# A planner's step times and due times reset, and some lower parts kept on VectorE, in a kernel of attention and two MLP layers

## The chip, the cores and the metric

The kernel runs on one core of a Trainium2 chip. The metric is the device time of one execution in microseconds. It has five engines here: TensorE (PE in the rows; its weight loads are PEld), VectorE (DVE), ScalarE (ACT), GpSimd (POOL) and SyncE (SP), which issues the DMAs. SBUF is the on-chip working memory, PSUM the memory that TensorE writes its products to, in banks.

## The reference

```python
def _attn_ref(q, k, v, g_q, g_k):          # (4, 12, 448, 64)
    q_n, k_n = rmsnorm(q, g_q), rmsnorm(k, g_k)
    scores = q_n @ k_n.T / sqrt(64)
    return softmax(scores) @ v

def _moe_ref(x, w_in, w_out):              # x: (1792, 768), w_in: (768, 2048), w_out: (2048, 768)
    h = x @ w_in
    return (h * sigmoid(h)) @ w_out

def _moe2_ref(x, w_in, w_out):
    return relu(x @ w_in) ** 2 @ w_out

def reference(**kwargs):
    x = attention of 4 batches and 12 heads, as (1792, 768)
    x = _moe_ref(x, moe_w_in, moe_w_out)
    return _moe2_ref(x, moe2_w_in, moe2_w_out)
```

Everything is float32.

## The kernel before

**Precision.** A float32 operand goes to TensorE as two parts: an upper part (a copy rounded to the matmul's type, `fp32r`, made by a CAST) and a lower part (what is left: the number less its upper part, a subtraction of two SBUF tiles, made by the helper `lower_part`, L558). One product takes three matmuls: upper by upper, upper by lower, lower by upper. In the tile names `gh` and `gl` are the upper and lower part of the hidden activations; `w`, `v`, `xb`, `yb`, `xc`, `part` and `W` hold both parts of weights, tokens and sums.

**Stages.** Attention over 24 pairs of heads takes the first 270 us and follows a fixed timetable. Then comes layer 1 (SiLU) until 736 us, in four quarters of the hidden columns; the first uses plain products (`up`, L1017, and `down`, L1201), the others a scheme with seven products in place of eight on half blocks (`seven`, L1104: nine matmuls of 448 columns in each product, into banks `t` or `pv`). Layer 2 (relu, squared) runs from 736 us. It handles the tokens in two halves, and in each half goes through eight groups of hidden columns: per group the products of the first matrix (L1104), the activation (ScalarE L1368 relu, L1374 square), the cast `gh` and the lower part `gl`, and then the second matrix into four `s` banks (384 columns, L1443) that VectorE adds to sums in SBUF (`acc`, L1462). In the second half, from 959 us on, the second matrix too uses seven products in most groups (class `products7`, L1568). For these the activation blocks are combined first into S1 to S4 (`h_sum`, L1500), and each of these sums is split by a cast (`h_hi`, on ScalarE or VectorE) and a lower part (`h_lo`) into tile `part` (S1, S2, S3) or `part` and `W` (S4). In TensorE's order of a group, product P4 (`s<-xb,gh`, nine matmuls) stands first, then P5 and P7 (`s<-xb,part`, nine each, from S1 and S3), then the others.

**What sets the order.** Apart from the attention's timetable, no order is written by hand. Each piece of work is a step with a set of engines that may do it, a time on each of them, and the steps that it needs. Class `Plan` makes the order: `forward` issues, of all steps that can go, the one that can start first, and of equal ones the one with the lower due time; `backward` works out due times from the end of that schedule; eight rounds, and the shortest schedule is issued. Table `DUE` adds an offset to the due time of each kind of step, by stage: `seg0` and `seg1` (layer 1 up to its second quarter and after), `end0` and `end1` (the two halves of layer 2, split at `self.turn`). The step times are formulas: `pe_t`, `dve_t`, `act_t`, `pool_t`, `any_t` (VectorE or GpSimd); `PROD` is one product of nine matmuls. An engine then works through its instructions strictly in the issued order, and waits on a semaphore where something that it needs is late.

**Names in the steps below.** `w_sum` (L1062, L1081) combines weight blocks in SBUF, `u_sum` (L1119) adds a product's bank to an SBUF tile, `join` (L1620) combines the sums at the end. Weights arrive as raw 8-byte words (`load_raw`, L913, L900), and ScalarE's `magnitude` and `low` (L920, L925) and VectorE's `merge` (L932) turn these into float32.

Of the kernel before, what the change touches and what calls it, by code (L numbers as in the profile page):

```python
# [98 lines left out]
class Step:  # L99
# [10 lines left out]
LAG = {"pe": 0.21, "act": 0.13, "dve": 0.12, "pool": 0.12, "sp": 1.9, "none": 0.0}  # L110
SELF = {"pe": 0.0, "act": 0.1, "dve": 0.1, "pool": 0.06, "sp": 1.9, "none": 0.0}
FORM = {"scores": "rows", "attend": "columns"}
SWITCH = 0.16
ENGINES = ("pe", "act", "dve", "pool", "sp", "none")
ROUNDS = 8
AHEAD = 25.0
DUE = {
    "end0": {"acc": 4.25, "down2": -1, "h_hi": 21.25, "h_lo": 3.75, "keep_parts2": -1.25, "load_y": -0.75, "p1_copy": 3.75, "prod": 0.25, "square": 1, "u_sum": -0.5, "w_hi2": -6, "w_lo2": -0.75, "w_sum": -0.75, "y_hi": 5.25, "y_lo": 4.25, "y_sum": -3.5},
    "end1": {"acc": 2, "down2": -11.25, "h_hi": 16, "h_lo": 2.5, "h_sum": -39.5, "join": 18, "keep_parts2": -11.75, "load_parts2": -2.25, "load_word2": 1.75, "load_y": 0.5, "p1_copy": 0.5, "prod": 2, "square": 21.25, "store": -1.25, "u_sum": -1, "w_hi2": 4.25, "w_sum": -4.5, "y_lo": -3, "y_sum": 2.5},
    "now": {"ident": 5.75, "swap_pools": -0.5},  # L120
    "seg0": {"add": -0.5, "down": 3, "g_hi": 0.5, "g_lo": 0.75, "keep": 10.25, "load_raw": -6, "load_y": 0.5, "low": 1, "magnitude": -2, "merge": -6, "out1": -1, "p1_copy": 4, "part": 0.5, "prod": 4.75, "silu": 0.5, "store_y": -1, "u_sum": 2.75, "up": 2.5, "w_hi": 4.5, "w_lo": 6.25, "w_sum": -2, "y_hi": 0.75, "y_lo": 1, "y_sum": 2},
    "seg1": {"add": -4.25, "down": -4.5, "g_hi": 2.25, "g_lo": 5, "keep2": 45.25, "load_raw2": 6, "load_word": -5.5, "load_y": -0.75, "low2": -1.5, "magnitude2": -3, "merge2": -4.5, "p1_copy": -6.25, "part": -3.75, "prod": -3.25, "silu": -5.75, "store_y": 7, "u_sum": 2.25, "w_hi": 1.75, "w_lo": 1, "w_sum": -3, "y_hi": 10, "y_lo": 0.75, "y_sum": 2.5},
}


class Plan:
# [47 lines left out]
    def link(self):  # L174


        for ring in self.rings.values():
            for b in ring:
                b.first = b.steps[0] if b.steps[0].nom is None else min(b.steps, key=lambda s: 1e9 if s.nom is None else s.nom)
                b.first.claims.append(b)  # L180
                if b.gate is not None:
                    b.first.needs[b.gate] = True
                for s in b.steps:
                    if s is not b.first:
                        s.needs.setdefault(b.first, False)
            ring.sort(key=lambda b: 1e9 if b.first.nom is None else b.first.nom)
            for n, b in enumerate(ring):
                b.turn = n
        pre = [dict() for _ in self.steps]
        for s in self.steps:  # L190
            for t, timed in s.needs.items():
                pre[s.n][t.n] = timed
            for b in s.claims:
                if b.turn:
                    t = b.ring[b.turn - 1].first
                    pre[s.n].setdefault(t.n, False)
                if b.turn >= b.n:
# [208 lines left out]
def kernel(  # L406
# [34 lines left out]
    step = plan.step  # L441
# [30 lines left out]
    def dve_t(n, rate=960.0, lock=False):  # L472
        return {"dve": (0.07 + n / rate, None, lock)}

    def pool_t(n, rate=474.0):
        return {"pool": (0.145 + n / rate, None, True)}

    def any_t(n, rate=474.0):
        return {**dve_t(n, 960.0, True), **pool_t(n, rate)}

    def copy_t(n):
# [2 lines left out]
    def pe_t(t):  # L484
        return {"pe": (t, None, False)}
# [13 lines left out]
    for n, src in enumerate((g_q, g_k)):  # L499
        for h in range(2):  # L500
# [4 lines left out]
                writes=[(graw, (n, h))],  # L505
# [10 lines left out]
    ident = sb([CP, CP], F32, "ident", 1)  # L516
# [35 lines left out]

        step(kind, when, copy_t(n), copy, reads=reads, writes=writes)

    def lower_part(kind, when, o, a, h, n, reads, writes, rate=474.0):

        step(
            kind, when, any_t(n, rate), lambda e: engine(e).tensor_tensor(o(), a(), h(), ALU.subtract),  # L558
            reads=reads, writes=writes,
        )  # L560

    def prepare(i):
# [88 lines left out]
        for n in range(2):  # L651
            n32 = sa([CP, NCH, 2, D], F32, "n")
            step(
                "norm", at, any_t(W2, 600.0),
                lambda e, n=n, n32=n32: engine(e).tensor_tensor(
                    n32.ap.rearrange("p c h d -> p h c d"),
                    qk.ap[:, n].rearrange("p (h c) d -> p h c d", h=2),
                    y.ap[:, n].rearrange("p (h c) -> p h c", h=2).unsqueeze(3).to_broadcast([CP, 2, NCH, D]),
                    ALU.mult),
                reads=[y, (qk, n)], writes=[n32],  # L660
            )
            plan.fix(i, "norm", j=n, at="dve" if i < 2 else "pool")
            pt = psum("t")

            def turn(e, n32=n32, pt=pt):
                for c in range(NCH):
                    nc.tensor.transpose(  # L667
                        pt.ap[:, c * CP:(c + 1) * CP], n32.ap[:, c].rearrange("p h d -> p (h d)"), ident.ap)

            step("turn_q", at, pe_t(0.384), turn, reads=[n32, ident], writes=[pt])  # L670
            plan.fix(i, "turn_q", j=n)

            def upper(e, n=n, pt=pt):
                o, a_ = T.ap[:, n, 0], pt.ap[:, :S]
# [32 lines left out]
    def weigh(i, T):  # L707
# [3 lines left out]
        for c in range(NCH):  # L711
# [15 lines left out]
            for j, pt in enumerate(pts):  # L727
                mx = sa([CP, 1], F32, "mx", 6)
                step(
                    "row_max", at, {"dve": (0.535, None, False)},  # L730
                    lambda e, pt=pt, mx=mx: nc.vector.tensor_reduce(  # L731
                        mx.ap, pt.ap[:CP, :S], AX.X, ALU.max, negate=True),
                    reads=[pt], writes=[mx],
                )
                plan.fix(i, "row_max", c, j)
                step(
                    "exp", at, {"act": (0.62, None, False)},
                    lambda e, j=j, c=c, pt=pt, mx=mx, E=E: nc.scalar.activation(  # L738
                        E.ap[:, j], pt.ap[:CP, :S], AF.Exp, bias=mx.ap, accum_out=sums.ap[:, j, c:c + 1]),
                    reads=[pt, mx], writes=[(E, j), (sums, (j, c))],  # L740
                )
                plan.fix(i, "exp", c, j)
                pe = psum("t")

                def turn(e, j=j, pe=pe, E=E):
                    for m in range(NCH):
                        nc.tensor.transpose(  # L747
                            pe.ap[:CP, m * CP:(m + 1) * CP], E.ap[:, j, m * CP:(m + 1) * CP], ident.ap)

                step("turn_e", at, pe_t(0.384), turn, reads=[(E, j), ident], writes=[pe])  # L750
                plan.fix(i, "turn_e", c, j)
                copy_step(
                    "e_copy", at, ECOPY[c][j], lambda c=c, j=j: PT[c // CT].ap[:, j * NCH:(j + 1) * NCH, c % CT, :],
                    lambda pe=pe: pe.ap[:CP, :S].rearrange("p (m t) -> p m t", t=CP), S, [pe], [(PT[c // CT], (c % CT, j))],
                )
                plan.fix(i, "e_copy", c, j)
        return PT, sums

    def attend(i, vr, PT, sums):
# [32 lines left out]
        for c2, pt in enumerate(PT):  # L792

            def products(e, c2=c2, pt=pt):
# [9 lines left out]
                        )  # L804

            step(
                "attend", at, pe_t(1.456), products,
                reads=[vr] + [(pt, (c, j)) for c in range(CT) for j in range(2)], writes=[(pv, c2)],
            )
            plan.fix(i, "attend", c2)  # L810
# [226 lines left out]
    FD = 2  # L1037
    halves = {}
    W3 = HC * P
    PROD = 9 * 0.2065  # L1040

    def view(b, a, c):

# [641 lines left out]
```

## Time and profile before

| | |
|---|---|
| median of 3 runs | 1165.32 us (1164.49, 1165.32, 1168.14) |
| the profiled execution | 1167.08 us |
| its span in the trace | 1165.3 us |
| TensorE busy | 1147.8 us, 99% of the span, 6817 matmuls |
| VectorE busy | 939.3 us, 81% |
| ScalarE busy | 632.3 us, 54% |
| GpSimd busy | 287.9 us, 25% |
| TensorE's granted clock, mean | 0.994 of full speed |

The busy share of a matmul includes its way through a pipeline, so that one matmul overlaps the next: the distance between the starts of two matmuls (their pitch) says how fast the engine goes. In the timeline one row can stand for several like instructions that follow each other (x2, x9); the bracket is the idle time of the engine ahead of it and what ended that. The code line is that of the helper which issues the instruction, so tiles tell more than lines.

### The profile page before, as it was taken

Reading aid. Unit: us, or ns where it says so; the run is one execution under the profiler, and the core shown is the slowest. Engines: PE = TensorE matmul, PEld = TensorE weight load, DVE = VectorE, ACT = ScalarE, POOL = GpSimd, SP = SyncE. Lnnn points to the kernel's source line nnn. Section 1 sums busy time; section 2 is a strip of 40 time slices with the busy share of each in tenths; the row PEclk is TensorE's granted clock in tenths of the full one; section 3 lists DMA queues with packets and bytes.
Section 4 is the critical chain, followed back from the end, with each engine's and each line's share of the span. In section 5 each row is a group of like instructions: output and inputs, shape, how many; then the busy total and the mean of one; then the engine's idle time right before and its main releaser. Section 6 shows DMA issues by size and latency. Waiting matters only on the chain.

```text
span 1165.3 us, 19244 instructions
## 1 busy us (share of the span) xinstructions
PE 1147.8 (99%) x6817; PEld 1018.8 (87%) x6817; DVE 939.3 (81%) x1685; ACT 632.3 (54%) x1290; POOL 287.9 (25%) x507
## 2 busy tenths in 40 slices
PE   7999999998999999999999999999999999999998
PEld 5777777777999999999999999999998999999997
DVE  7888888886876868996878698588888976888876
ACT  5999999985554444555535353543433535333321
POOL 4566676632000101210111021001121120122220
PEclk8999999999999999999999999999999999999999
DMA  6566768578855564778776849977777696555444
GB/s 175 94 103 115 105 109 111 99 125 175 275 167 185 172 212 133 263 236 273 244 238 209 272 145 329 337 271 261 286 264 260 217 378 230 177 176 190 164 163 135
DMA packets 142064, 235.22 MB, mean 202 GB/s; under 512 B 32016, under 2 KB 105744, under 8 KB 141968
## 3 DMA queue, kind: packets, MB, share of 16 engines
q1 hardware_dynamic: 141728, 233.80, 67.2%
q8 instruction: 54, 0.88, 0.3%
q14 instruction: 42, 0.34, 0.1%
q10 hardware_dynamic: 240, 0.20, 0.1%
HBM read 157.58 MB, written 76.37 MB: 201 GB/s over the span
## 4 chain that ended last, share of the span: by engine, by line
PE 91%; DVE 4%; ACT 2%; DMA 1%; issue 1%; SPq 0%; POOL 0%; ACTq 0%; DVEq 0%; POOLq 0%
PE t L1104 22%; PE s L1201 20%; PE s L1443 11%; PE pv L1104 9%; PE t L747 7%; PE pv L797 7%; PE s L720 6%; PE s L1568 6%; PE t L1017 2%; PE t L667 2%; DMA raw<-in_moe_w_out_dram 1%; DVE gg L1462 1%; DVE w L558 1%; DVE g L1119 0%; DVE g L1500 0%
## 5 line engine op out<-in xcount | busy, mean ns | idle before, releaser
L1201 PE MATMUL s<-gg,w 128*128 128x448 f32 x1152 | 240.4, 367 | 0.0
L1201 PEld LDWEIGHTS s<-gg,w 128*128 128x128 f32 x1152 | 216.2, 188 | 19.8 <-DVE g L1213 0.3
L1119 DVE TENSOR_TENSOR g<-t,g 128x448 f32<-128x448 f32 x180 | 108.8, 619 | 63.9 <-PE t L1104 53.1
L1443 PE MATMUL s<-w,gh 128*128 128x384 f32 (+1 forms) x564 | 143.0, 334 | 2.1 <-DVE gg L1462 1.1
L738 ACT ACTIVATE E<-s,mx 112x448 f32<-112x448 f32 x192 | 122.9, 653 | 13.7 <-ACT xf L537 7.9
L731 DVE TENSOR_REDUCE mx<-s 112x1 f32<-112x448 f32 x192 | 107.4, 611 | 14.4 <-PE s L720 14.1
L1462 DVE TENSOR_TENSOR gg<-s,gg 128x384 f32<-128x384 f32 (+1 forms) x197 | 102.6, 547 | 18.1 <-PE s L1443 17.7
L558 DVE TENSOR_TENSOR w<-W,w 128x768 fp32r<-128x768 f32 (+1 forms) x123 | 111.7, 917 | 4.2 <-ACT w L549 3.3
L1443 PEld LDWEIGHTS s<-w,gh 128*128 128x128 f32 x564 | 101.8, 188 | 4.0 <-DVE gg L1462 1.9
L1104 PE MATMUL t<-yb,w 128*128 128x448 f32 x468 | 103.1, 367 | 0.2 <-DVE w L558 0.2
L747 PEld LDWEIGHTS t<-ident,E 112*112 112x112 f32 x768 | 73.8, 134 | 32.5 <-issue 19.1
L549 ACT CAST w<-W 128x768 fp32r<-128x768 f32 (+1 forms) x74 | 54.9, 744 | 83.8 <-PE s L1201 31.9
L747 PE MATMUL t<-ident,E 112*112 112x112 f32 x768 | 94.7, 266 | 1.2 <-ACT E L738 1.2
L1368 ACT ACTIVATE g<-g 128x448 f32<-128x448 f32 x48 | 27.7, 578 | 124.6 <-DVE g L1119 124.1
L1443 PE MATMUL s<-w,gl 128*128 128x384 f32 (+1 forms) x282 | 94.3, 335 | 0.3 <-POOL gl L558 0.3
L1104 PEld LDWEIGHTS t<-yb,w 128*128 128x128 f32 x468 | 87.6, 188 | 8.1 <-DVE w L558 0.5
L797 PE MATMUL pv<-PT,vv 112*64 112x224 f32 x768 | 83.0, 359 | 0.1
L720 PE MATMUL s<-T 64*112 64x448 f32 x576 | 73.8, 388 | 1.3 <-ACT T L676 1.2
L1104 PE MATMUL pv<-xb,w 128*128 128x448 f32 x324 | 72.4, 367 | 0.0
L539 DVE COPY PT<-t 112x448 f32<-112x448 f32 x96 | 59.1, 618 | 11.6 <-PE t L747 11.5
L797 PEld LDWEIGHTS pv<-PT,vv 112*64 112x64 f32 x768 | 51.0, 136 | 20.0 <-ACT xf L537 0.3
L1104 PEld LDWEIGHTS pv<-xb,w 128*128 128x128 f32 x324 | 60.7, 188 | 5.5
(168 smaller groups left out, 2213.1 us busy)
## 6 DMA issues: line engine op xcount, KB each, us to landing
raw<-in_moe_w_in_dram SPq DMA_DIRECT2D x32, 768.0 KB
raw<-in_moe_w_out_dram SPq DMA_DIRECT2D x24, 512.0 KB
raw<-in_moe_w_out_dram SPq DMA_DIRECT2D x16, 768.0 KB
su<-w SPq DMA_DIRECT2D x16, 768.0 KB
w<-su SPq DMA_DIRECT2D x16, 768.0 KB
xf<-y SPq DMA_DIRECT2D x48, 224.0 KB
xf<-x SPq DMA_DIRECT2D x39, 224.0 KB
ki<-W SPq DMA_DIRECT2D x16, 384.0 KB
```

Source lines behind the costliest of these rows:

```text
L558: kind, when, any_t(n, rate), lambda e: engine(e).tensor_tensor(o(), a(), h(), ALU.subtract),
L720: nc.tensor.matmul(pts[j].ap[:CP, :S], T.ap[r, 0, a, c * CP:(c + 1) * CP], T.ap[r, 1, b_], start=(k_ == 0), stop=(k_ == 2),)
L731: lambda e, pt=pt, mx=mx: nc.vector.tensor_reduce(mx.ap, pt.ap[:CP, :S], AX.X, ALU.max, negate=True),
L738: lambda e, j=j, c=c, pt=pt, mx=mx, E=E: nc.scalar.activation(E.ap[:, j], pt.ap[:CP, :S], AF.Exp, bias=mx.ap, accum_out=sums.ap[:, j, c:c ...
L747: nc.tensor.transpose(pe.ap[:CP, m * CP:(m + 1) * CP], E.ap[:, j, m * CP:(m + 1) * CP], ident.ap)
L797: nc.tensor.matmul(pv.ap[j * D:(j + 1) * D, c2 * CT * CP:(c2 + 1) * CT * CP], vr.ap[:, j * NCH + m, :], pt.ap[:, j * NCH + m].rearrange("p ...
L1104: nc.tensor.matmul(pt.ap[:, :S], w_()[:, c0 + c, :], view(b, a, c)(), start=(start and c == 0 and k == 0), stop=(c == HC - 1 and k == 2), ...
L1119: lambda e: nc.vector.tensor_tensor(o.ap, pt.ap[:, :S], a.ap, ALU.add),
L1201: nc.tensor.matmul(pt.ap[:, :S], w_()[:, f, :], gg.ap[:, k, a, f, :], start=(f == 0 and n == 0), stop=(f == HQ - 1 and n == 2),)
L1443: nc.tensor.matmul(pt.ap[:, :en], g.ap[:, fi, c0:c0 + P], w_()[:, 0, e0:e0 + en], start=(n == 0), stop=(n == 5),)
L1462: "acc", at, dve_t(n), lambda e: nc.vector.tensor_tensor(o(), pt.ap[:, :n], o(), ALU.add),
L1568: nc.tensor.matmul(pt.ap[:, :NH], a[i][0](m), b[j][0](), start=(start and k == 0), stop=(k == 2), skip_group_check=True,)
```

## The change

All of it is in the planner's numbers and in one rule; the arithmetic is the same, and TensorE has as many matmuls as before.

- GpSimd's step time goes from 0.145 us and 474 elements per us to 0.1 us and 415 elements per us.
- `PROD` goes from 9 × 0.2065 to 9 × 0.2028 us; a turn of the attention from 0.384 to 0.406, an attended product from 1.456 to 1.512, and the time that a change of matmul form adds from 0.16 to 0.13. Since the nominal position of a step is made of such times, the point `self.turn` moves with them.
- A lower part of an activation (`h_lo`) in the last half of layer 2 can't go to GpSimd any more.
- All offsets of `DUE` are others.

```diff
-SWITCH = 0.16
+SWITCH = 0.13
...
 DUE = {
-    "end0": {"acc": 4.25, "down2": -1, "h_hi": 21.25, "h_lo": 3.75, "keep_parts2": -1.25, "load_y": -0.75, "p1_copy": 3.75, "prod": 0.25, "square": 1, "u_sum": -0.5, "w_hi2": -6, "w_lo2": -0.75, "w_sum": -0.75, "y_hi": 5.25, "y_lo": 4.25, "y_sum": -3.5},
+    "end0": {"acc": -0.5, "h_hi": 18.5, "h_lo": 3.25, "keep_parts2": 10.75, "load_word2": -0.5, "load_y": -0.75, "p1_copy": -1.75, "relu": -0.25, "square": 8.5, "u_sum": 2, "w_hi2": 1, "w_lo2": -0.5, "w_sum": 2.75, "y_hi": 3.5, "y_lo": -1, "y_sum": -4},
...
 }
@@ link
+        for s in self.steps:
+            if s.kind == "h_lo" and s.when[1] >= self.turn:
+                s.on.pop("pool", None)
+                s.at = "dve"
...
-    def pool_t(n, rate=474.0):
-        return {"pool": (0.145 + n / rate, None, True)}
+    def pool_t(n, rate=415.0):
+        return {"pool": (0.1 + n / rate, None, True)}
 
-    def any_t(n, rate=474.0):
+    def any_t(n, rate=415.0):
         return {**dve_t(n, 960.0, True), **pool_t(n, rate)}
...
-            step("turn_q", at, pe_t(0.384), turn, reads=[n32, ident], writes=[pt])
+            step("turn_q", at, pe_t(0.406), turn, reads=[n32, ident], writes=[pt])
...
-                step("turn_e", at, pe_t(0.384), turn, reads=[(E, j), ident], writes=[pe])
+                step("turn_e", at, pe_t(0.406), turn, reads=[(E, j), ident], writes=[pe])
...
-                "attend", at, pe_t(1.456), products,
+                "attend", at, pe_t(1.512), products,
...
-    PROD = 9 * 0.2065
+    PROD = 9 * 0.2028
```

The attention's order on TensorE is the same in both programs; from layer 1 on, runs of equal products change places, and helpers move between VectorE, GpSimd and ScalarE. Three places follow. The code lines of the changed kernel are higher by four from the new loop on (L1104 is L1108, L558 is L562, L1081 is L1085, L1443 is L1447, L1462 is L1466, L1500 is L1504, L1568 is L1572).

Place one, VectorE in the first half of layer 2, about 874 to 883 us in the trace of before: the weight sums, the lower parts and the bank sums that free the banks of a run `s<-w,gh` (L1443). Before:

```order
L1119 TENSOR_TENSOR g<-t,g 128x448
L1062 TENSOR_TENSOR W<-W 128x384
L551 CAST v<-W 128x384
L1062 TENSOR_TENSOR W<-W 128x384
L558 TENSOR_TENSOR gl<-g,gh 128x448
L1081 TENSOR_TENSOR W<-W 128x384
L1462 TENSOR_TENSOR gg<-s,gg 128x384
L1081 TENSOR_TENSOR W<-W 128x384
L558 TENSOR_TENSOR gl<-g,gh 128x448
L1462 TENSOR_TENSOR gg<-s,gg 128x384 x2
```

and now:

```order
L1123 TENSOR_TENSOR g<-t,g 128x448 x2
L1066 TENSOR_TENSOR W<-W 128x384
L1380 TENSOR_TENSOR g<-g 128x448
L1066 TENSOR_TENSOR W<-W 128x384
L562 TENSOR_TENSOR v<-W,v 128x384
L1085 TENSOR_TENSOR W<-W 128x384
L1466 TENSOR_TENSOR gg<-s,gg 128x384 x2
L562 TENSOR_TENSOR gl<-g,gh 128x448
L1085 TENSOR_TENSOR W<-W 128x384
L1466 TENSOR_TENSOR gg<-s,gg 128x384 x3
```

Two bank sums (L1462, now L1466) stand now right behind the first of the two `w_sum` L1081 (now L1085); before, `gl` stood ahead of that `w_sum`, and one bank sum behind it. The GpSimd instruction that ran beside the first `w_sum` (the lower part of `w`) is still issued there, after a `gl`; the lower part of `v` has moved from GpSimd to VectorE.

Place two, TensorE at about 929 to 932 us, where a run of the second matrix begins (`gh` and `gl` are the activations of the group). Before:

```order
L1104 MATMUL t<-xc,w 128x448 x9
L1104 MATMUL t<-part,w 128x448 x9
L1443 MATMUL s<-w,gh 128x384 x2
L1443 MATMUL s<-w,gl 128x384
L1443 MATMUL s<-w,gh 128x384 x2
```

and now:

```order
L1108 MATMUL t<-xc,w 128x448 x9
L1108 MATMUL t<-part,w 128x448 x9
L1108 MATMUL pv<-raw,w 128x448 x9
L1447 MATMUL s<-w,gh 128x384 x2
L1447 MATMUL s<-w,gl 128x384
```

A product of nine matmuls on `raw` and `w` now stands ahead of the first matmul that reads `gl`.

Place three, VectorE in the second group of the last half, about 985 to 991 us: the sums S1 and S2 (L1500), the bank sums and the lower parts in `part`. Before:

```order
L1500 TENSOR_TENSOR g<-g 128x384
L558 TENSOR_TENSOR gl<-g,gh 128x64
L1119 TENSOR_TENSOR g<-t,g 128x448
L1500 TENSOR_TENSOR g<-g 128x384
L1462 TENSOR_TENSOR gg<-s,gg 128x384
L558 TENSOR_TENSOR part<-g,part 128x384
L1462 TENSOR_TENSOR gg<-s,gg 128x384 x5
```

and now:

```order
L1504 TENSOR_TENSOR g<-g 128x384
L562 TENSOR_TENSOR gl<-g,gh 128x64
L1123 TENSOR_TENSOR g<-t,g 128x448
L1504 TENSOR_TENSOR g<-g 128x384
L1466 TENSOR_TENSOR gg<-s,gg 128x384 x3
L562 TENSOR_TENSOR part<-g,part 128x384 x2
```

The lower part of S1 comes two bank sums later, and that of S2, which GpSimd made, stands behind it. In the fifth group of that half the order on TensorE changes too. Before, nine products on `raw` stood between P4 and P5:

```order
L1568 MATMUL s<-xb,gh 128x384
L1568 MATMUL s<-W,gh 128x384
L1568 MATMUL s<-xb,gl 128x384
L1104 MATMUL pv<-raw,w 128x448 x9
L1568 MATMUL s<-xb,part 128x384 x18
L1568 MATMUL s<-w,gh 128x384 x2
```

and now P5 follows P4, and they come behind it:

```order
L1572 MATMUL s<-xb,gh 128x384
L1572 MATMUL s<-W,gh 128x384
L1572 MATMUL s<-xb,gl 128x384
L1572 MATMUL s<-xb,part 128x384 x9
L1108 MATMUL pv<-raw,w 128x448 x9
L1572 MATMUL s<-xb,part 128x384 x9
```

## Rows read from the trace of the kernel before

**Rows 1.** Page: busy time, the chain that ended last, one costly group

```profile
PE 1147.8 (99%) x6817; PEld 1018.8 (87%) x6817; DVE 939.3 (81%) x1685; ACT 632.3 (54%) x1290; POOL 287.9 (25%) x507
...
PE 91%; DVE 4%; ACT 2%; DMA 1%; issue 1%; SPq 0%; POOL 0%; ACTq 0%; DVEq 0%; POOLq 0%
...
L1119 DVE TENSOR_TENSOR g<-t,g 128x448 f32<-128x448 f32 x180 | 108.8, 619 | 63.9 <-PE t L1104 53.1
```

**Rows 2.** Windows: length; busy us (count) of PE, PEld, DVE, ACT, POOL; PE clock, DMA share, GB/s

```profile
265.00:300.00 35.00, 31.92 (x174) 27.40 (x171) 21.01 (x35) 17.80 (x33) 4.23 (x3) 0.95 0.79 187
300.00:736.00 436.00, 436.00 (x2131) 399.52 (x2130) 348.78 (x587) 215.25 (x349) 50.11 (x35) 1.00 0.69 227
870.00:885.00 15.00, 13.58 (x70) 12.14 (x69) 15.00 (x21) 6.47 (x12) 5.02 (x4) 1.00 0.74 272
960.00:1126.00 166.00, 164.83 (x862) 154.53 (x861) 132.84 (x260) 64.41 (x124) 31.52 (x30) 1.00 0.55 194
```

**Rows 3.** TensorE's waits: us in total, times, longest us

```profile
PE t L1017 <- ACT g L1029: 3.0, 1, 3.0
...
PE s L1568 <- DVE part L558: 1.1, 2, 0.8
```

**Rows 4.** Chain of waits: start us, us, engine and line, count

```profile
306.78 26.04 PE s L1201 x126
...
512.00 5.64 PE t L1104 x27
...
529.80 24.32 PE s L1201 x120
```

**Rows 5.** Timeline 270 to 284 us: start, length, work [idle before]

```profile
280.20 0.66 ACT L920 ACTIVATE W<-raw 128x512 f32<-128x512 f32 x1 [7.97 <-DMA raw<-in_moe_w_out_dram]
...
283.31 2.58 PE L1017 MATMUL t<-xc,w 128*128 128x448 f32 x9 [3.00 <-ACT g L1029]
```

**Rows 6.** Timeline 870 to 882 us: VectorE beside GpSimd

```profile
870.97 2.77 DVE L558 TENSOR_TENSOR w<-W,w 128x768 fp32r<-128x768 f32 x2
...
871.59 1.34 POOL L558 TENSOR_TENSOR gl<-g,gh 128x448 fp32r<-128x448 f32 x1 [0.96 <-ACT gh L549]
...
878.24 1.83 POOL L558 TENSOR_TENSOR w<-W,w 128x768 fp32r<-128x768 f32 x1 [0.35 <-ACT w L549]
878.29 2.20 DVE L1081 TENSOR_TENSOR W<-W 128x384 f32<-128x384 f32 x1
...
881.01 0.61 PE L1443 MATMUL s<-w,gh 128*128 128x384 f32 x2 [1.13 <-DVE gg L1462]
```

**Rows 7.** Timeline at 930 us: TensorE waits for a lower part

```profile
930.17 1.30 POOL L558 TENSOR_TENSOR gl<-g,gh 128x448 fp32r<-128x448 f32 x1 [2.47 <-issue]
...
930.70 0.52 PE L1443 MATMUL s<-w,gh 128*128 128x384 f32 x2
...
931.52 0.45 PE L1443 MATMUL s<-w,gl 128*128 128x384 f32 x1 [0.30 <-POOL gl L558]
```

**Rows 8.** Timeline 988 to 992 us: the second group of products

```profile
988.31 0.55 DVE L558 TENSOR_TENSOR part<-g,part 128x384 fp32r<-128x384 f32 x1
...
988.55 1.18 POOL L558 TENSOR_TENSOR part<-g,part 128x384 fp32r<-128x384 f32 x1 [33.52 <-ACT part L549]
988.77 2.41 DVE L1462 TENSOR_TENSOR gg<-s,gg 128x384 f32<-128x384 f32 x5
...
988.91 3.06 PE L1568 MATMUL s<-xb,part 128*128 128x384 f32 x16 [0.82 <-DVE part L558]
```

**Rows 9.** Timeline 1068 to 1073 us: the fifth group

```profile
1068.39 0.55 DVE L558 TENSOR_TENSOR part<-g,part 128x384 fp32r<-128x384 f32 x1
...
1068.79 1.17 POOL L558 TENSOR_TENSOR gl<-g,gh 128x448 fp32r<-128x448 f32 x1 [1.78 <-ACT gh L549]
...
1069.21 3.48 PE L1568 MATMUL s<-xb,part 128*128 128x384 f32 x18
1069.33 1.04 DVE L1500 TENSOR_TENSOR g<-g 128x384 f32<-128x384 f32 x1
```

More of the change, by code (lines that the diff above doesn't have):

```diff
@@ L117 @@
 DUE = {
-    "end0": {"acc": 4.25, "down2": -1, "h_hi": 21.25, "h_lo": 3.75, "keep_parts2": -1.25, "load_y": -0.75, "p1_copy": 3.75, "prod": 0.25, "square": 1, "u_sum": -0.5, "w_hi2": -6, "w_lo2": -0.75, "w_sum": -0.75, "y_hi": 5.25, "y_lo": 4.25, "y_sum": -3.5},
-    "end1": {"acc": 2, "down2": -11.25, "h_hi": 16, "h_lo": 2.5, "h_sum": -39.5, "join": 18, "keep_parts2": -11.75, "load_parts2": -2.25, "load_word2": 1.75, "load_y": 0.5, "p1_copy": 0.5, "prod": 2, "square": 21.25, "store": -1.25, "u_sum": -1, "w_hi2": 4.25, "w_sum": -4.5, "y_lo": -3, "y_sum": 2.5},
@@ L120 @@
-    "now": {"ident": 5.75, "swap_pools": -0.5},
-    "seg0": {"add": -0.5, "down": 3, "g_hi": 0.5, "g_lo": 0.75, "keep": 10.25, "load_raw": -6, "load_y": 0.5, "low": 1, "magnitude": -2, "merge": -6, "out1": -1, "p1_copy": 4, "part": 0.5, "prod": 4.75, "silu": 0.5, "store_y": -1, "u_sum": 2.75, "up": 2.5, "w_hi": 4.5, "w_lo": 6.25, "w_sum": -2, "y_hi": 0.75, "y_lo": 1, "y_sum": 2},
-    "seg1": {"add": -4.25, "down": -4.5, "g_hi": 2.25, "g_lo": 5, "keep2": 45.25, "load_raw2": 6, "load_word": -5.5, "load_y": -0.75, "low2": -1.5, "magnitude2": -3, "merge2": -4.5, "p1_copy": -6.25, "part": -3.75, "prod": -3.25, "silu": -5.75, "store_y": 7, "u_sum": 2.25, "w_hi": 1.75, "w_lo": 1, "w_sum": -3, "y_hi": 10, "y_lo": 0.75, "y_sum": 2.5},
+    "end0": {"acc": -0.5, "h_hi": 18.5, "h_lo": 3.25, "keep_parts2": 10.75, "load_word2": -0.5, "load_y": -0.75, "p1_copy": -1.75, "relu": -0.25, "square": 8.5, "u_sum": 2, "w_hi2": 1, "w_lo2": -0.5, "w_sum": 2.75, "y_hi": 3.5, "y_lo": -1, "y_sum": -4},
@@ new lines @@
+    "end1": {"acc": -4.5, "down2": -20.25, "h_hi": 15.25, "h_lo": 3.75, "h_sum": -5, "join": -0.75, "load_parts2": 0.5, "load_word2": -5.25, "load_y": 2.75, "p1_copy": 2, "prod": -0.75, "square": 50.25, "store": -3.75, "u_sum": 4, "w_hi2": -3.25, "w_lo2": -19.25, "w_sum": -2, "y_hi": -2.75, "y_lo": -0.25, "y_sum": -8.75},
+    "now": {"ident": 7.5, "swap_pools": -3},
+    "seg0": {"add": -0.75, "down": 4, "g_hi": 3, "g_lo": 2, "keep": -4.5, "load_raw": -29.75, "low": 6, "magnitude": 6.25, "merge": -5.5, "out1": 1.75, "p1_copy": 3, "part": -1, "prod": 5, "silu": -2.25, "store_y": -0.25, "u_sum": 2.75, "up": -1.75, "w_hi": 7.25, "w_sum": 6, "y_hi": -15, "y_lo": -0.25, "y_sum": -2.5},
@@ L123 @@
+    "seg1": {"add": -1, "down": -5.75, "g_hi": 6.5, "keep2": 55.75, "load_raw2": -0.25, "load_word": 7.75, "load_y": -0.5, "low2": 24.5, "magnitude2": 2.25, "merge2": -5.75, "out1": -1.75, "p1_copy": 1.25, "part": 11.5, "prod": -4, "silu": -11.5, "u_sum": 1.75, "w_hi": -2.5, "w_lo": 1.75, "y_hi": 6.25, "y_lo": -1.5, "y_sum": 10.75},
 }
@@ L553, in upper_part, with lower_part @@
         step(kind, when, copy_t(n), copy, reads=reads, writes=writes)
-    def lower_part(kind, when, o, a, h, n, reads, writes, rate=474.0):
+    def lower_part(kind, when, o, a, h, n, reads, writes, rate=415.0):
         step(
```

## The prediction

> **What bounds the kernel now.** I read the page first. TensorE is busy for 1147.8 of 1165.3 us, and the chain that ended last is TensorE for 91% [rows 1]. So only two things can move the time: the 17.5 us in which TensorE does nothing, and the pace at which it works. GpSimd's 25% and VectorE's 81% count only where TensorE waits for them. The list of TensorE's waits comes next: the largest behind the attention is one of 3.0 us at the start of layer 1, then the lower parts of the sums S1 (1.1 us in two places) [rows 3]. Then I cut the span into windows at the stages: from 300 to 736 us, which is layer 1 without its start, TensorE is never idle; the idle time stands at the start of layer 1 (35.00 − 31.92 = 3.1 us), in one stretch of the first half of layer 2 (870 to 885: 1.4 us) and in small pieces in the last half (960 to 1126: 1.2 us) [rows 2].
>
> The chain of waits shows the pace. 126 matmuls of layer 1 take 26.04 us, which is 206.7 ns from one to the next, and 120 of the same line take 24.32, which is 202.7 [rows 4]. The turn is the run that starts at 512.00: 27 matmuls in 5.64, 208.9 each, just behind a short wait for a bank; all runs of the chain behind it up to 736 have the quicker pace. The granted clock is 1.00 at both. So layer 1 ran about half at either pace, as its mean says: 436.00 us for 2131 matmuls are 204.6 ns [rows 2]. The reason isn't in the trace, and the order of instructions doesn't tell which pace a kernel gets.
>
> **The change, part by part.** The profiled execution took 1167.08 us, 1.8 more than its span and 1.76 above the median 1165.32; I work in its time and take 1.76 off at the end.
>
> Attention: TensorE's order is unchanged, its fixed timetable too. 0.
>
> Start of layer 1. TensorE waits because silu, which empties a bank, stands on ScalarE behind the conversion of a weight block that lands at about 280.2 (ScalarE idle for 7.97 us ahead of it); TensorE goes on at 283.31 after 3.00 us [rows 5]. In the new order the same two conversions and the table load still stand ahead of silu. 0, with −3 (the block lands in time) and +3 (a DMA is put ahead of it) as bounds.
>
> First half of layer 2, place one. At 878.24 GpSimd begins a lower part of 1.83 us, and VectorE's `w_sum`, begun at 878.29, takes 2.20 instead of the 0.55 that a subtraction of that size takes elsewhere [rows 6, 8]: it is held until GpSimd has ended. The bank sums behind it come late, and TensorE loses 1.13 at 881.01. A smaller loss ahead of it is of the same kind: two lower parts of `w` take 2.77 on VectorE beside GpSimd's `gl` (1.34). In the new order two bank sums stand right behind the first `w_sum`, so a VectorE held later holds back no bank before the fourth group of six matmuls, and the earlier `gl` has left GpSimd. The window's idle time is 15.00 − 13.58 = 1.42 us [rows 2], and refilling the pipeline after a wait costs about 0.17 more each (below). Of about 1.7 I count 1.6 as gone: **−1.6** (bounds: 0, if GpSimd's two instructions, now back to back, hold VectorE at another place; −1.8).
>
> Here a rule can be weighed against the row. The Trainium skill (SBUF — State Buffer, Who interferes with whom) says that a VectorE instruction with two inputs in SBUF and a GpSimd instruction that reads SBUF share a port pair, and that the later one is blocked until the earlier has ended. This trace agrees: 878.29 + 2.20 = 880.49 is 1.83 behind 878.24 plus about 0.4 [rows 6]. The rule also speaks against the change: four `h_sum` and six more `w_sum` now go to GpSimd, and each may hold VectorE for up to its own length. By that alone VectorE would lose up to 10 us (an estimate: ten times about 1.0, the GpSimd time of 384 columns being 1.18 in rows 8); by the rows only what a bank sum or an S1 waits for reaches TensorE.
>
> Place two. At 930.70 two matmuls start, and the third, which reads `gl` from GpSimd (930.17, 1.30 us), starts 0.82 later instead of 2 × 0.173 = 0.35 (0.173 is the pitch of 384 columns: 18 take 3.48 in rows 9, less the tail) [rows 7]. The loss is 0.47, of which 0.30 is idle and 0.17 the refilled pipeline. Now nine matmuls (9 × 0.2067 = 1.86 us) stand ahead of it. **−0.5**; nothing takes its place, since `gl` is then over a microsecond early.
>
> Last half of layer 2: seven groups with P4, P5, P7. P4's nine matmuls take 1.56 us, and the third of P5 needs the lower part of S1, so that this has to be ready 1.9 us after P4's start unless other products stand between. A further 384-column instruction on VectorE costs (2.41 − 0.55)/4 = 0.465 us [rows 8].
> - Group 2: two bank sums more ahead of the lower part, which ends at 988.31 + 0.55 now: 2 × 0.465 = **+0.9** on a wait that already costs 0.82 + 0.17.
> - Group 1: same order on TensorE, one more cast of 384 columns on ScalarE ahead of what it waits for. No row shows such a cast; I take an estimate of about VectorE's time for that size: **+0.4** (bounds 0 and 0.9).
> - Group 5: before, nine products on `raw` covered P5 (it began 0.17 late at 1069.21). Now they come behind P5's first nine. VectorE has to do `u_sum` (0.62 [rows 1]), `h_sum`, three bank sums, a small `gl` (0.14, estimated from its 64 columns) and the lower part: 0.4 + 0.54 + 5 × 0.465 + 0.14 = 3.4 against the 1.9 needed. A wait of 1.5 takes the place of 0.4: **+1.1**.
> - Groups 3, 4, 6, 7: fills of nine products stand between P4 and P5 or P5 and P7, as in group 5 before. There `h_sum` took 1.04 beside GpSimd's `gl` (1068.79, 1.17) instead of 0.55 [rows 9], and the groups lost 0.1 to 0.4. GpSimd's lower parts are gone there, so the holding goes with them: **−1.1** for the four.
>
> Together +1.3. VectorE gets 14 more lower parts of 384 columns (6.5 us), about five `gl` (2.7) and five small ones (0.7), and loses four `h_sum` (1.9): 8.0 us more over seven groups, 1.1 each. It was busy for 132.84 of 166.00 us there [rows 2]; with this about 84%. The cover is the 5 us that it is idle in a group.
>
> Other small waits of layer 2 (two of under 0.5, one near 1145) stand behind the same work in both orders: 0, ±0.5. Pace: 0.
>
> Sum: −1.6 − 0.5 + 1.3 = −0.8. 1167.08 − 0.8 − 1.76 = **1164.5 us**, no change that this measurement can tell: that takes over 0.3%, 3.5 us.
>
> **Rivals.**
> 1. *Layer 1 at the slow pace to its end.* The short wait at 512 came from a bank sum behind other work on VectorE; in the new order that sum (`u_sum`, L1119) stands ahead of it, so this wait may be missing and the pace not turn. 2131 × 206.7 ns = 440.4 in place of 436.0: +4.4, 1168.9. Against it: any other short wait does the same.
> 2. *Layer 1 at the quick pace from its start.* 2131 × 202.7 = 431.9: −4.1, 1160.4. For it: the 3.00 us wait is just ahead. Against it: in this trace that wait was followed by the slow pace.
> 3. *Nearly all waits of layer 2 go*, since GpSimd's times are now nearer to its rows (1.17 for 448 columns in rows 9 against 0.145 + 448/474 = 1.09 planned). Then the +2.4 of groups 1, 2, 5 don't come and 1.4 more go: 1160.7. Against it: the new order shows these groups' lower parts late.
> 4. *VectorE becomes the bound of the last half.* If the lower part of S1 is later than 1.9 us after P4's start in all seven groups, each waits 1.5: 10.5 in place of the 5.2 that my sum holds: +1.3 on a loss of 3.9 before (1.1 in groups 1 and 2 each, 0.1 in 3, 0.4 in each of 4 to 7, counted along the timeline as in rows 8 and 9). That is +5.3, and 1169.8. For it: 84% busy, the two groups above. Against it: the fills in four groups.
> 5. *The start of layer 1 moves* by up to 3 us either way: 1161.5 or 1167.5.
>
> **How the numbers follow.** Forecast 0.44 (within 0.3% 0.37, faster 0.05, slower 0.02), rival 1 0.17 (slower 0.09, same 0.08), rival 2 0.15 (faster 0.14), rival 3 0.11 (faster 0.10), rival 4 0.10 (slower), rival 5 0.03. Faster 0.30, same 0.47, slower 0.23. The range runs from below rivals 2 and 3 (each less a microsecond of the unknown waits) to rival 4: 1159.0 to 1169.8.
>
> **What would show it.** The chain of the changed kernel should have TensorE without idle time at 870 to 885 and at 930; waits of `s<-xb,part` for `part` of about 1.5 to 2 us in groups 1, 2 and 5 and of nearly nothing in the others; `w_sum` on VectorE without a 2.20; the 3.0 us of L1017 as before. The pace of L1201 says which of rivals 1 and 2 is there. I am wrong if those three waits are missing or stand in all groups, if new waits appear in layer 1, or if the mean of the 2131 matmuls leaves 204.6 by more than a nanosecond.

## The result and the profile after

The changed kernel takes 1172.51 us (median of 11 runs, 1166.39 to 1183.60), the kernel before beside it 1165.44 (11 runs, 1159.56 to 1169.30). The ratio is 1.0061, with a 95% interval of 1.0035 to 1.0088: slower by 0.6%, and above the range that was predicted (1159.0 to 1169.8). The profiled execution took 1169.55 us, 2.5 more than that of before, with a span of 1167.7.

The page of the changed kernel, as [rows 1]: TensorE's busy time and its share of the chain are lower.

```profile
PE 1146.3 (98%) x6817; PEld 1022.5 (88%) x6817; DVE 943.4 (81%) x1703; ACT 630.7 (54%) x1292; POOL 260.5 (22%) x487
...
PE 85%; ACT 5%; DMA 4%; DVE 4%; issue 1%; SPq 0%; POOL 0%; DVEq 0%; ACTq 0%; POOLq 0%
```

The windows of the changed kernel (length; busy us and count of PE, PEld, DVE, ACT, POOL; granted clock of TensorE, share of the DMA engines, GB/s), with one more than in [rows 2], 925 to 960, and layer 1 to 728 only, since it ends earlier here:

```profile
300.00:728.00 428.00, 427.66 (x2106) 394.83 (x2105) 354.34 (x595) 204.99 (x335) 34.52 (x27) 1.00 0.71 229
870.00:885.00 15.00, 15.00 (x86) 14.84 (x85) 12.44 (x22) 4.97 (x9) 3.06 (x2) 1.00 0.87 332
925.00:960.00 35.00, 30.81 (x157) 29.27 (x156) 24.26 (x41) 9.61 (x20) 9.73 (x9) 0.95 0.93 326
960.00:1126.00 166.00, 162.38 (x844) 153.05 (x843) 132.50 (x264) 66.08 (x126) 17.40 (x13) 0.99 0.53 187
```

Place one is clean: 15.00 of 15.00 us busy at 870 to 885, where 13.58 were. But from 925 to 960 TensorE is idle for 4.2 us and works at a granted clock of 0.95, and in the last half 3.6 us are idle instead of 1.2. The first window says that layer 1 was quicker in this execution: 2106 matmuls in 427.66 us are 203.1 ns each, where [rows 2] give 204.6.

TensorE's waits, as [rows 3] (us in total, times, longest):

```profile
PE pv L1108 <- ACT xc L553: 4.2, 1, 4.2
...
PE s L1572 <- DVE part L562: 2.9, 3, 1.8
PE t L1021 <- ACT g L1033: 2.1, 1, 2.1
...
PE s L1572 <- ACT gg L1463: 0.4, 1, 0.4
PE t L1108 <- DVE g L1123: 0.3, 1, 0.3
```

The first is new, and the largest of the program. The timeline around it, in the changed kernel:

```profile
917.90 4.18 SPq L1249 DMA_DIRECT2D xf<-y  x4
...
918.61 2.65 POOL L562 TENSOR_TENSOR xb<-xf,xb 128x448 fp32r<-128x448 f32 x1 [20.87 <-ACT xb L553]
...
922.18 0.38 SPq L960 DMA_DIRECT2D w<-sw  x1
922.61 0.42 SPq L973 DMA_DIRECT2D su<-w  x1
...
923.10 2.02 PE L1108 MATMUL t<-part,w 128*128 128x448 f32 x9
923.29 0.32 SPq L960 DMA_DIRECT2D w<-sz  x1
...
929.30 3.23 PE L1108 MATMUL pv<-raw,w 128*128 128x448 f32 x9 [4.19 <-ACT xc L553]
...
932.33 0.84 PE L1447 MATMUL s<-w,gh 128*128 128x384 f32 x2
```

The product `pv<-raw` at 929.30 is that of place two, which the new order puts ahead of the run. It needs the matmuls' weights `w<-sw` (768 KB), which SyncE issues at 922.18; its predecessor ends near 925.0. The list gives ScalarE's `xc` as what released it. That cast stands behind the product in the program's order, so it can't be; it only ends at the same moment. The product's other operand, `raw`, was done at 914.8, and the trace's semaphore events have the last of the load's sixteen parts landed at 929.17, 0.13 us before the product starts. A second profile of the same kernel names the load (below). Behind the wait, nine matmuls take 3.23 us in place of 2.02 (rows 923.10 and 929.30): the granted clock is 0.50 from 930 to 933. Against the pitch of before, all of this costs 6.0 us.

The load is also issued late. Its buffer is free when `pv<-xb`, three products ahead, has ended (921.4), but SyncE issues in order, and of the four `xf<-y` ahead of it the third waits until 921.29 for GpSimd's lower part `xb`, begun at 918.61, which takes 2.65 us. That is at most 0.8 us of the wait; no run took it away.

In the trace's stretches (from the first matmul of one to that of the next), this execution against the one of before: attention +1.0, layer 1 −3.8 (the pace), layer 2 up to its last seven groups +2.4, these groups +3.0, the rest −0.2; together +2.4, the spans' difference.

### The profile page after: what moved, and what is told of

The parts are those of the page before. It is cut to its first block, busy times and chain, and to the rows that moved or that the text cites. A ratio compares the mean times of both kernels' runs of the same rounds, so it can differ in the third digit from the quotient of the medians.

```text
span 1167.7 us, 19157 instructions
## 1 busy us (share of the span) xinstructions
PE 1146.3 (98%) x6817; PEld 1022.5 (88%) x6817; DVE 943.4 (81%) x1703; ACT 630.7 (54%) x1292; POOL 260.5 (22%) x487
## 4 chain that ended last, share of the span: by engine, by line
PE 85%; ACT 5%; DMA 4%; DVE 4%; issue 1%; SPq 0%; POOL 0%; DVEq 0%; ACTq 0%; POOLq 0%
PE t L1108 22%; PE s L1205 20%; PE s L1447 12%; PE pv L1108 9%; PE s L1572 6%; PE t L751 5%; PE pv L801 4%; PE s L724 4%; PE t L1021 2%; ACT E L742 2%; DMA ki<-W 1%; PE t L671 1%; DMA R<-rd 1%; DVE gg L1466 1%; ACT PT L541 1%
## 5 line engine op out<-in xcount | busy, mean ns | idle before, releaser
L1123 DVE TENSOR_TENSOR g<-t,g 128x448 f32<-128x448 f32 x180 | 109.3, 620 | 62.7 <-PE t L1108 56.9
L1447 PE MATMUL s<-w,gh 128*128 128x384 f32 (+1 forms) x564 | 143.0, 334 | 0.7 <-DVE gh L555 0.7
L1466 DVE TENSOR_TENSOR gg<-s,gg 128x384 f32<-128x384 f32 (+1 forms) x197 | 103.7, 551 | 30.6 <-PE s L1447 29.5
L562 DVE TENSOR_TENSOR w<-W,w 128x768 fp32r<-128x768 f32 (+1 forms) x123 | 108.1, 887 | 3.8 <-ACT w L553 2.9
L1447 PEld LDWEIGHTS s<-w,gh 128*128 128x128 f32 x564 | 102.3, 189 | 2.1 <-DVE gh L555 1.1
L1108 PE MATMUL t<-yb,w 128*128 128x448 f32 x468 | 102.9, 366 | 0.0
L1447 PE MATMUL s<-w,gl 128*128 128x384 f32 (+1 forms) x282 | 94.2, 334 | 0.0
L1108 PEld LDWEIGHTS t<-yb,w 128*128 128x128 f32 x468 | 87.6, 188 | 7.0
L553 ACT CAST w<-W 128x768 fp32r<-128x768 f32 (+1 forms) x64 | 47.4, 740 | 78.5 <-PE s L1205 16.7
L1108 PE MATMUL pv<-xb,w 128*128 128x448 f32 x324 | 72.0, 366 | 0.0
L929 ACT ACTIVATE raw<-raw 128x768 int32<-128x768 uint16 (+1 forms) x72 | 59.8, 830 | 11.2 <-DMA raw<-in_moe_w_out_dram 8.1
```

What stands on the lines that cost most here:

```text
L1108: nc.tensor.matmul(pt.ap[:, :S], w_()[:, c0 + c, :], view(b, a, c)(), start=(start and c == 0 and k == 0), stop=(c == HC - 1 and k == 2), ...
L1123: lambda e: nc.vector.tensor_tensor(o.ap, pt.ap[:, :S], a.ap, ALU.add),
L1447: nc.tensor.matmul(pt.ap[:, :en], g.ap[:, fi, c0:c0 + P], w_()[:, 0, e0:e0 + en], start=(n == 0), stop=(n == 5),)
L1466: "acc", at, dve_t(n), lambda e: nc.vector.tensor_tensor(o(), pt.ap[:, :n], o(), ALU.add),
```

## The experiments

Two theories stood against each other and against a third. W: the loss is the product of place two, which waits for weights that come late, with the fall of the clock behind it. D: the loss is VectorE's work in the last half, by its order (D') or its amount (V). P: the difference is only the pace of layer 1. In the edits `order` is the list of steps that the planner issues; a step is moved in it by hand, so that everything else keeps its order (the code below gives names in place of the steps' numbers).

For each profile the table shows the time of layer 1 (2250 matmuls), that of stretch A (layer 2 up to the first P4, 1168 matmuls) and that of B (962 matmuls: the seven groups from there on and the first products of the eighth), so that the same number of matmuls is timed in each kernel. These times leave out what another stretch did in the same execution. The time of layer 1 holds the pace that this execution had.

| kernel | ratio to before (95%) | layer 1 | A | B |
|---|---|---|---|---|
| before | | 465.8 | 222.5 | 185.5 |
| before, again | | 458.7 | 222.4 | 185.4 |
| changed | 1.0061 (1.0035 to 1.0088) | 462.0 | 224.9 | 188.5 |
| changed, again | 1.0052 (1.0030 to 1.0074) | 465.8 | 226.5 | 187.0 |
| product back | 1.0032 (1.0012 to 1.0052) | 463.9 | 222.4 | 187.0 |
| S1 first | 1.0072 (1.0044 to 1.0100) | 465.3 | 225.1 | 187.2 |
| both of these | 1.0027 (1.0000 to 1.0053) | 460.5 | 222.4 | 187.2 |
| stores later | 1.0022 (1.0001 to 1.0043) | 461.1 | 223.0 | 187.0 |
| given back | 1.0046 (1.0020 to 1.0072) | 463.4 | 223.1 | 187.5 |
| rule alone | 1.0057 (1.0036 to 1.0079) | 463.5 | 226.1 | 187.0 |
| due times alone | 1.0076 (1.0049 to 1.0102) | 465.3 | 223.7 | 188.2 |
| times and rule | 1.0112 (1.0080 to 1.0144) | 464.4 | 230.5 | 187.1 |
| all but the rule | 1.0152 (1.0117 to 1.0187) | 462.8 | 228.3 | 190.8 |
| before, bank sums first | 0.9997 (0.9968 to 1.0027) | 462.9 | 221.3 | 186.3 |

**The product back behind the run.**

```diff
+# prod: the product pv<-raw of place two, copy: the copy of its bank
+move(order, prod, before=first_product_behind_the_run)
+move(order, copy, before=first_product_behind_the_run)
```

> The changed kernel with one product moved: the nine matmuls pv<-raw that stand ahead of the run of 84 plain matmuls in the first half of layer 2 go behind that run, with the copy of their bank. Theory W (the product waits for weights that a DMA brings late, and the clock falls behind the wait): the 4.2 us wait near 925 us goes, the matmuls behind it run at full clock, and the time falls by 5 to 6 us against the changed kernel, to about 1167. Rival D (the lower parts on VectorE in the last half are the loss): the wait is only passed on to a later product, under 2 us gained. Rival P (the loss is the pace of layer 1, another one in each execution): no difference in the median beyond 1 us.

A falls to 222.4, that of the kernel before, and the ratio from 1.0061 and 1.0052 to 1.0032. So about half of the loss is made there. But the run that now stands in the product's place waits too; in TensorE's waits of this kernel:

```profile
PE s L1452 <- DVE gl L567: 1.1, 1, 1.1
PE s L1452 <- DVE gg L1471: 0.8, 1, 0.8
PE s L1452 <- ACT gh L558: 0.8, 1, 0.8
```

The lower part `gl`, the cast `gh` and a bank sum of this run are late as well in the new order. W holds in the place, and not in the whole price: about 3 us of the 6 stay.

**The lower part of S1 first.**

```diff
+# groups 2 and 5: the lower part of S1 ahead of the bank sums
+move(order, lower_S1[2], before=bank_sum[2])
+move(order, lower_S1[5], before=bank_sum[5])
```

> The changed kernel with the lower part of S1 put ahead of the bank sums on VectorE in groups 2 and 5 of the last half. Theory D' (the order on VectorE makes these waits): the wait of group 2 falls from 2.1 to about 1.1 us, the clock no longer falls behind it (another 1.4), and that of group 5 from 1.5 to about 0.8; together -3.2 us against the changed kernel, about 1169.5. Theory W predicts the same here and leaves the 4.2 us near 925. Rival P: within 1 us of the changed kernel.

No gain: B is 187.2, as that of the changed kernel without a fall of the clock (187.0). The second group in this kernel:

```profile
989.51 0.55 DVE L567 TENSOR_TENSOR part<-g,part 128x384 fp32r<-128x384 f32 x1
...
989.98 1.48 DVE L1471 TENSOR_TENSOR gg<-s,gg 128x384 f32<-128x384 f32 x3
...
990.11 2.31 PE L1577 MATMUL s<-xb,part 128*128 128x384 f32 x10 [0.36 <-DVE part L567]
...
992.91 1.31 PE L1577 MATMUL s<-xb,part 128*128 128x384 f32 x6 [0.48 <-DVE gg L1471]
```

The wait for `part` is down from 1.75 to 0.36 us, and ten matmuls further on TensorE waits 0.48 for the bank sums, which are now behind it; against the pitch the group still loses about 2 us. D' falls: VectorE has no idle time here from 988.4 to 994, and its order only says where TensorE waits.

**Both.**

```diff
+move(order, prod, before=first_product_behind_the_run)
+move(order, copy, before=first_product_behind_the_run)
+move(order, lower_S1[2], before=bank_sum[2])
+move(order, lower_S1[5], before=bank_sum[5])
```

> Both of the two edits before. If W and D' both hold they add up: -8.5 to -9 us against the changed kernel, about 1164, which would be a little faster than the kernel before (1165.4). If the waits only move on, less than 5 us.

1.0027, the same as the product alone within the intervals; the second edit adds nothing.

**The stores later.**

```diff
+# keep_a, keep_b: the two stores su<-w at 922.6 and 923.7 us
+move(order, keep_a, before=later_weight_load)
+move(order, keep_b, before=later_weight_load)
```

> The changed kernel with the product left where it is, and two stores of weight parts (768 KB each) issued by SyncE after the two weight loads that follow them instead of ahead of these. Theory W with its price in bandwidth (the late load shares the DMA engines with the stores issued right behind it): the load that the product waits for lands 1 to 3 us earlier, the wait of 4.2 falls to 1.5 to 3, and with under 2 us of idle time the clock may stay up: -2 to -4 us against the changed kernel. If the load is late for its own latency or for its issue alone, no change there.

The load and the product in the timeline of this kernel:

```profile
919.51 0.38 SPq L965 DMA_DIRECT2D w<-sw  x1
...
922.88 0.88 SPq L978 DMA_DIRECT2D su<-w  x2
...
924.85 3.52 PE L1113 MATMUL pv<-raw,w 128*128 128x448 f32 x9 [2.41 <-DMA w<-sw]
```

From the issue of the load to the product it is 5.3 us (919.51 to 924.85) instead of 7.1 (922.18 to 929.30), the wait 2.41 instead of 4.19, and the ratio 1.0022. So the stores that SyncE issued right behind the load took part of its bandwidth. The other profiles agree: by the semaphore events this load lands 5.2 us after its issue in the two kernels with the stores later, 5.7 where the first store is issued 2.0 us behind it (times and rule), and 6.7 to 8.2 in the eleven profiles where that is 0.4 to 0.5 us. The kernel before is one of the eleven (6.7), but there the product comes 12 us after the landing. The clock fell here too, behind 2.41 us: the nine matmuls take 3.52 us. The rest remains: the buffer that this load fills becomes free with the product three ahead, so that it can't be issued more than about 3.7 us (two products) before its own product is due, and it takes 5.3 even now.

**Parts of the change alone.** The first is the kernel before with the new rule, the second with the new table, the third the changed kernel with the old table, the fourth without the rule.

```diff
+            if s.kind == "h_lo" and s.when[1] >= self.turn:   # rule alone
...
+    "end0": {"acc": -0.5, "h_hi": 18.5, ...                    # due times alone
...
-    "end0": {"acc": -0.5, "h_hi": 18.5, ...                    # times and rule
...
-            if s.kind == "h_lo" and s.when[1] >= self.turn:   # all but the rule
```

> The kernel before with the new rule alone: lower parts of the last half on VectorE, old step times, old due times. In its order the product pv<-raw stands behind the run at 930 us, as before. Theory W (the loss is that product, waiting for weights): no loss there, so the whole kernel within 0.1% of before, but for what VectorE does in the last half. Theory V (in that half VectorE itself is late where it has the lower parts, whatever their order): P5 directly follows P4 in groups 1, 2, 4 and 6, with waits of 1.5 to 2 us in each in place of 1.1, 1.1, 0.4 and 0.4: +3 to +4 us, ratio 1.003.

> The kernel before with the new due times alone (old step times, GpSimd may do lower parts). In its order the product pv<-raw stands behind the run, and in groups 3 to 7 nine products stand between P4 and P5. Theory W: no wait of 4 us near 925, ratio 0.998 to 1.002. Theory V: no waits for part in groups 3 to 7 beyond 0.4 us. If the due times are the loss: ratio 1.005 or more.

> The changed kernel with the old due times. Its order has the product pv<-raw ahead of the run, as the changed kernel. Theory W: a wait of 3 to 4.5 us near 925 with the fall of the clock behind it, and the waits of theory V in the groups where P5 follows P4 (1, 2, 4, 5, 7): ratio 1.005 to 1.008. If the due times are the loss: 1.002 or less.

> The changed kernel without the rule (GpSimd may do lower parts of the last half). Its order has the product pv<-raw ahead of the run, and fills between P4 and P5 in groups 3 to 7. Theory W: the wait near 925 of 3 to 4.5 us and the clock behind it stay, +4 to +6 us against before. Theory V: the waits of groups 2 and 5 go back to 1.1 and 0.4, -2 to -3 us against the changed kernel; ratio 1.003 to 1.005.

The product stands ahead of the run in the last two, which have the new step times, and there TensorE waits for the same load; in the third:

```profile
PE pv L1108 <- DMA w<-sw: 3.0, 1, 3.0
```

and in the fourth:

```profile
PE pv L1104 <- DMA w<-sw: 4.9, 1, 4.9
```

The first two keep the product behind the run and have no such wait, as W has it. But they are slower than before all the same (W had them within 0.2%), by waits elsewhere that no theory had. The kernel with the rule alone:

```profile
PE s L1447 <- DVE gl L562: 2.3, 2, 1.9
...
PE pv L1108 <- ACT g L1372: 2.2, 1, 2.2
```

and that with the due times alone, most of it in layer 1:

```profile
PE t L1104 <- DVE w L551: 2.3, 2, 1.7
PE s L1443 <- DVE gh L551: 1.9, 1, 1.9
```

Both have the quick pace of 202.7 ns through nearly all of layer 1, as the second profile of before has (458.7 us), and take 463.5 and 465.3 us for it. The last two miss their ratios as well: 1.0112 where at most 1.008 was expected, and 1.0152 where 1.003 to 1.005 was. In the fourth GpSimd may have the lower parts of the last half again, and by V its B had to fall by 2 to 3 us; it is 190.8, the longest of all.

So the loss belongs to no one part. The rule alone, the due times alone, and either of them with the new step times each let the planner make another order of the whole program, and each of these orders has waits that the planner's times did not hold. The new step times alone were not run.

**Work given back to GpSimd.**

```diff
+# on top of the stores later and S1 first, in groups 1, 2 and 5:
+at[lower_S2] = at[lower_gl] = "pool"
```

> The changed kernel with the stores later (as stores_later), the lower part of S1 first in groups 2 and 5, and the lower parts of S2 and of the activation block behind it given back to GpSimd in groups 1, 2 and 5. Theory V (VectorE has more to do there than its time, so only taking work off it helps, not its order): the waits fall from 1.5, 2.1 and 1.5 to about 1.1, 1.1 and 0.8 us, -2 us against stores_later (about 1161.5, the time before). Theory D' (the order): it fell with s1_first, where the sum of the waits stayed. If GpSimd's hold on VectorE eats what is given back: no change against stores_later.

B is 187.5: nothing gained. The second group in this kernel:

```profile
987.71 1.15 POOL L569 TENSOR_TENSOR gl<-g,gh 128x448 fp32r<-128x448 f32 x1
987.79 1.49 DVE L1511 TENSOR_TENSOR g<-g 128x384 f32<-128x384 f32 x1
...
989.80 1.32 PE L1579 MATMUL s<-xb,part 128*128 128x384 f32 x6 [0.97 <-DVE gg L1473]
```

VectorE's `h_sum` takes 1.49 us beside GpSimd's `gl`, in place of 0.55: what VectorE is spared here, it loses by being held. V, that work taken off VectorE helps, is not shown; this way of taking it off does not help.

**The changed kernel again, the kernel before again.** Nothing is edited in either.

> The changed kernel once more, beside the others on one chip. Theory W: the wait for weights near 925 is there again with 3.5 to 5 us, and the ratio is 1.005 to 1.008. Rival P (the pace of layer 1 makes the difference of the medians): the pace turns at another point in this execution than at 287 and 686 us, and the ratio is under 1.004.

> The kernel before once more, for its pace: if the turn from 206.7 to 202.7 ns at 512 us is the order's, it stands there again; if it is the execution's, layer 1 turns elsewhere or not at all, and takes 460 to 469 us instead of 465.8. The waits of layer 2 stand where they were.

The changed kernel has the wait again, longer, and here the trace names the load:

```profile
PE pv L1108 <- DMA w<-sw: 4.6, 1, 4.6
PE s L1572 <- DVE part L562: 2.9, 3, 1.8
```

The ratio is 1.0052 though layer 1 took 465.8 in its profile, 3.8 more than in the first. And the kernel before, again, has the quick pace from about 281 us on (window 300 to 728 us):

```profile
300.00:728.00 428.00, 428.00 (x2112) 396.05 (x2111) 346.39 (x585) 213.08 (x346) 50.75 (x35) 1.00 0.70 228
```

That is 202.7 ns for each of 2112 matmuls, where the first profile had 204.6. The same program takes 458.7 or 465.8 us for layer 1. So P is right in that the pace belongs to the execution and moves single runs, and it doesn't explain the loss: A and B repeat within 0.1 us in the kernel before, and are longer in the changed one in both profiles.

**The kernel before with its bank sums first.**

```diff
+# at 878 us: two bank sums ahead of the held w_sum, a third ahead of gl
+move(order, w_sum, before=next_w_sum); move(order, bank_sum_2, before=w_sum)
+move(order, bank_sum_3, before=gl)
```

> The kernel before with a hand edit taken from the changed order at place one: the bank sums ahead of the w_sum that GpSimd holds near 878 us. By the reading of the traces (the held w_sum keeps the bank sums behind it from freeing banks) the 1.8 us near 880 go, -1.6 us, ratio 0.9986; if the loss there is only handed on, 1.000.

A falls by 1.2 us (222.5 to 221.3), as read from the trace. B was 0.8 longer in this execution, and the ratio 0.9997 can't tell either from nothing. No version was found that beats the kernel before.

## Why the prediction was wrong

**Place two** is the step that failed: "**−0.5**; nothing takes its place, since `gl` is then over a microsecond early." I looked at what the run behind the nine matmuls gains and not at what these nine need themselves. They read weights that a DMA brings, and by SyncE's order that load is issued 2.8 us before its product is due (922.18 against 925.0). In place of −0.5 it costs 6.0 us against the pitch (7.5 in the second profile), where the kernel before lost 0.6. Beyond the start of layer 1 the prediction named no DMA.

**Place one** (−1.6): right in its mechanism, and a little more than its bound of −1.8. GpSimd's lower part still holds VectorE, now for a `gl`, but the two bank sums are done before it; in the changed kernel's timeline:

```profile
872.99 0.55 DVE L1466 TENSOR_TENSOR gg<-s,gg 128x384 f32<-128x384 f32 x1
...
873.94 0.56 DVE L1466 TENSOR_TENSOR gg<-s,gg 128x384 f32<-128x384 f32 x1 [0.40 <-PE s L1447]
874.05 1.85 POOL L562 TENSOR_TENSOR w<-W,w 128x768 fp32r<-128x768 f32 x1
...
874.41 1.97 DVE L562 TENSOR_TENSOR gl<-g,gh 128x448 fp32r<-128x448 f32 x1
```

There is no wait of TensorE behind it, and the 2.2 us that the kernel before lost there against the pitch are gone.

**The seven groups** (+1.3): right in size. B is +1.6 where the clock stayed (187.0 against 185.4). Group 2, for which I said 0.9 more than 0.82 + 0.17:

```profile
987.88 1.48 DVE L1466 TENSOR_TENSOR gg<-s,gg 128x384 f32<-128x384 f32 x3
...
989.27 1.02 DVE L562 TENSOR_TENSOR part<-g,part 128x384 fp32r<-128x384 f32 x2
...
989.88 4.31 PE L1572 MATMUL s<-xb,part 128*128 128x384 f32 x16 [1.75 <-DVE part L562]
```

1.75 idle after three bank sums, with about 0.2 for the refill: 1.9 predicted. Behind it, 16 matmuls take 4.31 us and not 3.06 [rows 8]: in this execution the clock fell here too, which cost 1.4 us, and in the changed kernel's second profile it did not. Against the pitch group 1 loses 1.5 in place of 1.1 (+0.4 was said), group 5 loses 1.5, groups 3, 6 and 7 nothing, as said; group 4 loses 0.45, where my sum left about 0.2 for the four. By the rule of the Trainium skill (SBUF — State Buffer, Who interferes with whom) the holding had to go with GpSimd's lower parts; it did in these groups, and the run that gave work back brought it back (1.49 against 0.55). What I said of VectorE's load does not hold: not 8.0 us more, but 132.50 in place of 132.84 in the window 960 to 1126, and 2.1 more over the same matmuls (156.0 against 153.9), so that the 84% that spoke for rival 4 were not there.

**The start of layer 1** (0): the wait is 2.1 and 2.3 us in the two profiles of the changed kernel, 3.0 and 1.8 in those of before. Unchanged within its scatter.

**The pace** (0, rivals 1 and 2): by the execution, not by the kernel. The quick pace from the start, rival 2, came in the second profile of before; in the changed kernel's first it held from 287 to 686 us, and its mean of 203.1 there left 204.6 by more than the nanosecond that I had set as a sign of being wrong. In its second profile the slow pace held to about 512, as in the first of before; no profile had it from the start to the end of layer 1, as rival 1 did. As rivals the paces were priced about rightly (the two profiles of before differ by 7.1 us in layer 1, of which about 5 is the pace and the rest the start) and meant wrongly: they tell single executions apart, and no run here ties a pace to a kernel.

**The sum.** The trace's stretches A and B give +2.4 and +4.1 for A, +3.0 and +1.6 for B, so +5.4 and +5.7; the ratio says 6 to 7. My sum had −2.1 for A and +1.3 for B. The miss lies in A, at place two, but for the 1.4 us of the clock behind group 2 in the first profile. Against it, the small waits of before near 772 and 820 us (0.6 against the pitch), which I had left at 0, are gone. Of what then is missing (0.3 to 1.7 us), 0.5 is a new wait in layer 1, for a bank that VectorE frees near 510 us (the 0.3 of `PE t L1108 <- DVE g L1123` above, with the refill), another sign of being wrong that I had set; what is left of it is open.

## What to carry to other kernels

When a reordered instruction closes a gap, look at all that the moved instruction itself reads, back to the DMA's issue, and at when the buffer of that DMA becomes free; a gap filled with work whose operands are later than the gap is a longer gap. Where an engine has no idle time in a stretch, its order only chooses who waits. And a scheduler's order is good as a whole: two of its inputs changed alone, and each with the third, all gave slower orders here, by waits that none of the inputs names.

## What the runs showed of the hardware

- The pitch of a 448-column matmul has two values, 206.7 and 202.7 ns, at a granted clock of 1.00. It can turn in the midst of layer 1, at places that differ between executions of one program, and mostly holds then for a hundred microseconds and more. Of the 14 turns in the 14 profiles (the start of layer 1 left out), 10 stand at a matmul that came 0.09 us or more late; there are 64 such among some 30 000, and most left the pace as it was. In layer 2, where runs of 448 and 384 columns alternate, its mean was 206.2 to 206.4 in every profile. What sets the pace is open.
- The granted clock fell behind waits of very different length: behind 4.19 and 2.41 us, and in one execution behind 1.75 but not in another behind the same wait of that kernel. Where it fell, nine matmuls of 448 columns took 3.23 us instead of 2.02.
- A load of 768 KB landed 5.2 us after its issue where stores of 768 KB came 3.4 us and more behind it, and 6.7 to 8.2 where one was issued 0.4 to 0.5 behind it.
- The holding works both ways: GpSimd's lower part of 448 columns at 918.61 took 2.65 us beside three lower parts on VectorE, instead of 1.17 [rows 9].
